# Weight conversion of a three-stage layer pair: whole tiles, sums on VectorE, and a held second layer

## The chip, the cores and the metric

The kernel runs on one core of one Trainium2 chip. The metric is the device time of one execution in microseconds (us). Before the change it is 1002.57 us, the median of 3 runs (1000.18 to 1002.59).

## The reference, cut to what matters

A linear attention gives x of 2304 tokens by 512, and two gated layers follow it. All data is float32.

```python
q_s = softmax(q, over d);  k_s = softmax(k, over s)      # 4 batches, 8 heads, 576 tokens, d = 64
x = (q_s @ (k_s^T @ v)) -> [2304, 512]
g = x @ w_gate; x = (g * sigmoid(g) * (x @ w_val)) @ w_out       # layer 0: 512 -> 1536 -> 512
x = ((x @ w_a) * (x @ w_b)) @ w_out2                             # layer 1: 512 -> 1536 -> 512
```

## The kernel before, in words

**Numbers as pairs.** TensorE multiplies operands of a shortened float format (fp32r). So every float32 operand is split into a high part (the rounded value, written by a cast on ScalarE) and a low part (the rest, a subtraction on VectorE or GpSimd), and every product takes three matmuls. x becomes `xhl`, the gated product becomes `h`, the weights become `w`.

**Where the weights come from.** Each weight matrix lies in HBM as 64-bit words, of which the kernel reads both 32-bit halves as integers. A part of the weights goes through a conversion of eight instructions (lines 367 to 388): on ScalarE `Abs` of the high words into `a` (L367, which VectorE may do instead, L369) and a scaling of the low words in place (L371); on VectorE a clamp (L373), a shift and mask (L376) and a merge with the sign (L379); then an exact integer sum of `a` and the low words (L384, on GpSimd, or on VectorE); then the cast to the high part of `w` on ScalarE (L302) and the subtraction to the low part of `w` (L296). The raw words are called `wr`.

**Tiles.** The 1536 hidden columns are 12 tiles of 128. Tile f of a layer holds 128 columns of both first matrices and 128 rows of the third: 1536 converted columns per partition. It is converted in two halves of 768 columns (tile 0 of layer 0 in three thirds of 512). Raw words of a half lie in one of the buffers `wr0`, `wr1` and, for most of layer 0, `xraw`; those of tiles 1 to 4 of layer 0 lie whole in tile buffers that are still free, so that they are loaded early. `a` has three buffers `a0`, `a1`, `a2` of one half each. A converted tile of layer 1 goes where the same tile of layer 0 was.

**Blocks.** The tokens are five blocks: four of 512 and a last one, block 4, of 256 (the rest rows of all four batches). Layer 0 runs blocks 0, 1, 2, 4, 3, layer 1 runs 0 to 4. In a block, each tile f gives two products `u` (24 matmuls, L743; L728 for the very first tile), and then, one tile later, `acc` takes the third product (12 matmuls, L770 or L773). Between them ScalarE makes `s` from the first product (L754), VectorE multiplies (L757), ScalarE casts to `h` (L302) and VectorE subtracts for its low part (L296). The two `u` products use two PSUM buffers; one is free again when `s` has read it, the other when the low part of `h` has been written. Block 0 of layer 0 is the one in which tiles are converted while they are used, and in which the attention of batch 1 also runs (four groups; `tm`, `kx`, `kr`, `kb`, `ut`, `kv`, `qt`, `ql`, `xt`, `xl` are its steps).

**Order.** All instructions are handed to a planner (class `Plan`), each with an engine, a cost, buffers that it reads and writes, and perhaps a due time or a second engine (`other`). The planner works due times back from the end (`prepare`, L95), then fills each engine in turn with what is ready and most urgent (`order`, L115). What it gives is a fixed queue for each engine, and every engine works its queue strictly in order. A step with a second engine goes there if the planner expects it to finish sooner (L140). The planner lets only one of VectorE and GpSimd work at a time for steps marked `port` (L136). Loads are issued by SyncE (SP) and are chained in the order in which they are written (`load`, L311). The conversion of layer 1 is written at L849, ahead of layer 1's first block, and the planner may start its loads and its steps up to the sum whenever buffers are free.

## Time and profile before

| | before |
|---|---|
| median of 3 runs | 1002.57 us |
| the profiled execution | 1002.42 us, of which 1000.5 us is the span |
| TensorE busy | 961.3 us (96%), mean granted clock 0.99 |
| VectorE, ScalarE, GpSimd busy | 402.0, 409.2, 172.2 us |
| sums on GpSimd (L384) | 48 of 49 |

The span runs from the first to the last instruction. "Busy" counts what an engine spends in an instruction, also while the instruction itself is held up. An entry in square brackets in a timeline is the idle time of the engine ahead of the instruction, with what ended it. Blocks of layer 0 begin at about 33 us (block 0), 172 us (block 1), 396 us (block 4) and 451 us (block 3).

### The profile page before, as it was taken

To read this page: it belongs to the slowest core of one execution; us is meant where nothing else is said; L and a number is where in the kernel's file an instruction comes from. 1 tells how busy PE (TensorE), PEld (TensorE's weight loads), DVE (VectorE), ACT (ScalarE), POOL (GpSimd) and SP (SyncE) were. 2 spreads that over 40 slices of the span, in tenths; PEclk is the share of its full clock that TensorE was granted. 3 is DMA by queue.
4 is the path that set the end of the run, shared out by engine and by line. 5 is a ranking of instruction groups with operands and counts; after the bars stand their busy time and mean duration, and the time that the engine had idled before them with its cause. 6 is when DMAs were issued, how large, how long until landed. Compare 5 with 4: busy or idle time off the path is not lost.

```text
span 1000.5 us, 12235 instructions
## 1 busy us (share of the span) xinstructions
PE 961.3 (96%) x4616; PEld 796.3 (80%) x4616; DVE 402.0 (40%) x693; ACT 409.2 (41%) x796; POOL 172.2 (17%) x193
## 2 busy tenths in 40 slices
PE   5699899999999999999999999999999999999997
PEld 4477677888888888898888888888888888888897
DVE  7988885332333233324566761211122112211211
ACT  5898986554454544223445441211121112111211
POOL 5655442100000001100444440000000000000000
PEclk9989899999999999999999999999999999999999
DMA  9825533211121114402334630010010001000100
GB/s 274 283 72 152 171 120 116 77 48 48 37 96 48 48 48 133 143 1 65 125 127 129 209 95 1 24 61 1 1 48 38 1 0 51 13 1 1 43 1 22
DMA packets 77138, 74.19 MB, mean 74 GB/s; under 512 B 29976, under 2 KB 64280, under 8 KB 76184
## 3 DMA queue, kind: packets, MB, share of 16 engines
q1 hardware_dynamic: 71416, 69.36, 22.4%
q10 hardware_dynamic: 5664, 4.07, 1.3%
q8 instruction: 36, 0.59, 0.3%
q14 instruction: 22, 0.18, 0.1%
HBM read 60.29 MB, written 13.11 MB: 73 GB/s over the span
## 4 chain that ended last, share of the span: by engine, by line
PE 83%; DMA 4%; ACT 4%; SPq 3%; DVE 2%; POOL 2%; issue 1%; POOLq 0%; DVEq 0%; ACTq 0%
PE u L743 53%; PE acc L773 15%; PE acc L770 12%; POOL a L384 2%; DMA ut<-in_k_dram 1%; DMA wr<-in_moe_w_gate_dram 1%; DMA wr<-in_moe_w_out_dram 1%; SPq L345 1%; PE kv L616 1%; PE xt L677 1%; DVE a L379 1%; SPq L504 1%; ACT L754 1%; ACT L601 1%; ACT a L367 0%
## 5 line engine op out<-in xcount | busy, mean ns | idle before, releaser
L743 PE MATMUL u<-xhl,w 128*128 128x512 f32 (+1 forms) x2856 | 624.4, 373 | 11.2 <-DVE w L296 7.2
L743 PEld LDWEIGHTS u<-xhl,w 128*128 128x128 f32 x2856 | 498.8, 189 | 109.4 <-DVE w L296 9.8
L757 DVE TENSOR_TENSOR u<-s,u 128x512 f32<-128x512 f32 (+1 forms) x120 | 77.1, 642 | 411.1 <-PE u L743 383.6
L754 ACT ACTIVATE s<-u 128x512 f32<-128x512 f32 (+1 forms) x120 | 66.8, 557 | 274.6 <-PE u L743 274.2
L770 PE MATMUL acc<-h,w 128*128 128x512 f32 (+1 forms) x720 | 165.2, 376 | 1.1 <-ACT ob L786 0.8
L773 PE MATMUL acc<-w,h 128*128 128x512 f32 x648 | 157.4, 392 | 0.0
L770 PEld LDWEIGHTS acc<-h,w 128*128 128x128 f32 x720 | 123.9, 188 | 28.5 <-issue 1.9
L302 ACT CAST h<-u 128x512 fp32r<-128x512 f32 (+1 forms) x120 | 65.0, 542 | 190.2 <-DVE u L757 188.0
L773 PEld LDWEIGHTS acc<-w,h 128*128 128x128 f32 x648 | 120.9, 188 | 25.6
L384 POOL TENSOR_TENSOR a<-a,wr 128x768 uint32<-128x768 uint32 (+1 forms) x48 | 95.2, 1984 | 177.5 <-DVE a L379 162.2
L296 DVE TENSOR_TENSOR h<-u,h 128x512 fp32r<-128x512 f32 (+1 forms) x120 | 76.3, 636 | 55.7 <-ACT h L302 55.5
L296 POOL TENSOR_TENSOR xhl<-xraw,xhl 128x512 fp32r<-128x512 f32 (+1 forms) x6 | 7.2, 1196 | 354.0 <-ACT xhl L302 239.9
L379 DVE SCALAR_TENSOR_TENSOR a<-wr,a 128x768 uint32<-128x768 uint32 (+1 forms) x49 | 52.0, 1062 | 0.5
L754 ACT ACT_TABLE_LOAD x26 | 33.4, 1283 | 29.2 <-PE u L743 29.0
L371 ACT ACTIVATE wr<-wr 128x768 uint32<-128x768 uint32 (+1 forms) x49 | 43.9, 897 | 3.0 <-DMA wr<-in_moe_w_out_dram 3.0
L302 ACT CAST w<-a 128x768 fp32r<-128x768 f32 (+1 forms) x49 | 39.9, 816 | 10.1 <-POOL a L384 6.2
L367 ACT ACTIVATE a<-wr 128x768 f32<-128x768 f32 (+1 forms) x38 | 33.7, 893 | 19.0 <-DMA wr<-in_moe_w_out_dram 15.2
L296 DVE TENSOR_TENSOR w<-a,w 128x768 fp32r<-128x768 f32 (+1 forms) x37 | 39.1, 1061 | 5.6 <-ACT w L302 4.0
L373 DVE TENSOR_SCALAR a<-a 128x768 f32<-128x768 f32 (+1 forms) x49 | 31.2, 639 | 20.7 <-ACT a L367 20.5
L376 DVE TENSOR_SCALAR a<-a 128x768 uint32<-128x768 uint32 (+1 forms) x49 | 30.3, 623 | 0.8
L296 POOL TENSOR_TENSOR w<-a,w 128x768 fp32r<-128x768 f32 (+1 forms) x12 | 22.5, 1875 | 17.4 <-ACT w L302 17.4
L601 ACT ACTIVATE ua<-uq,st 128x64 f32<-128x64 f32 (+1 forms) x72 | 24.6, 344 | 0.1
(107 smaller groups left out, 451.7 us busy)
## 6 DMA issues: line engine op xcount, KB each, us to landing
wr<-in_moe_w_out_dram SPq DMA_DIRECT2D x46, 256.0 KB, 4.4
xraw<-x SPq DMA_DIRECT2D x7, 1024.0 KB
wr<-in_moe_w_a_dram SPq DMA_DIRECT2D x24, 256.0 KB, 2.9
wr<-in_moe_w_b_dram SPq DMA_DIRECT2D x24, 256.0 KB, 3.0
wr<-in_moe_w_gate_dram SPq DMA_DIRECT2D x22, 256.0 KB, 5.8
wr<-in_moe_w_val_dram SPq DMA_DIRECT2D x22, 256.0 KB, 4.6
x<-ob SPq DMA_DIRECT2D x16, 256.0 KB, 2.1
out_dram<-ob SPq DMA_DIRECT2D x16, 256.0 KB, 3.4
```

The source lines that it names most:

```text
L296: engine.tensor_tensor(out=out(), in0=x(), in1=y(), op=op)
L302: add("scalar", act_us(n), lambda: nc.scalar.copy(out=hi(), in_=src()), [src_key], [hi_key])
L367: add("scalar", act_us(e) + 0.08, lambda: nc.scalar.activation(out=a().bitcast(F32), in_=high().bitcast(F32), func=AF.Abs), parts, [a], ot ...
L371: add("scalar", act_us(e) + 0.08, lambda: nc.scalar.activation(out=low(), in_=low(), func=AF.Copy, scale=2.0 ** -29), parts, [(raw, (h, "l ...
L379: add("vector", dve_us(e), lambda: nc.vector.scalar_tensor_tensor(out=a(), in0=high(), scalar=0xC0000000, in1=a(), op0=ALU.bitwise_and, op ...
L384: engine.tensor_tensor(out=a(), in0=a(), in1=low(), op=ALU.add)
L601: add("scalar", act_us(width) + 0.1, lambda: nc.scalar.activation(out=out(), in_=qraw()[:, at:at + width], func=AF.Exp, bias=st()[:, 0, x: ...
L743: nc.tensor.matmul(ps()[:, 0:n], lhsT=wv[:, c, :], rhs=x()[:, xs, c, 0:n], start=(a == 0 and c == 0), stop=(a == 2 and c == KD - 1))
L754: add("scalar", act_us(n), lambda: nc.scalar.activation(out=s()[:, 0:n], in_=ga()[:, 0:n], func=AF.Silu if l == 0 else AF.Copy), [ga], [s] ...
L757: add("vector", dve_us(n), lambda: nc.vector.tensor_tensor(out=gb()[:, 0:n], in0=s()[:, 0:n], in1=gb()[:, 0:n], op=ALU.mult), [s, gb], [gb])
L770: nc.tensor.matmul(ps()[:, 0:n], lhsT=w()[:, 4 + ws, o * P:(o + 1) * P], rhs=h()[:, hs, 0:n], start=begin, stop=end)
L773: nc.tensor.matmul(ps(), lhsT=h()[:, hs, o * P:(o + 1) * P], rhs=w()[:, 4 + ws, :], start=begin, stop=end)
```

## The change

A tile of layer 0 with number 1 to 4 is now converted whole: clamp, shift, merge, sum, cast and subtraction are one instruction each over 1536 columns, and so are `Abs` and the scaling. Such a tile's `a` has 1536 columns and lies in `a0` or in `xraw`; the third `a` buffer is gone, so that halves have `a0` and `a1`. The integer sum has VectorE as its first engine and GpSimd as its second. The first load of layer 1 gets an order (`hold`) behind the first product of block 3 of layer 0, which does not count for due times; as all loads are chained, all of layer 1's loads lie behind it.

```diff
     def add(self, engine, cost, fn, reads=(), writes=(), due=None, after=(), table=None, nbytes=0, other=None,
-            port=None):
+            port=None, hold=()):
...
-        deps, order, allocs = set(), set(after), []
+        deps, order, allocs = set(), set(after) | set(hold), []
...
             for s in self.succ[n]:
+                if n in ops[s]["hold"]:
+                    continue
...
     def load(fn, nbytes, writes, issue=0.475):
-        n = dma(fn, nbytes, [], writes, after=last_load, issue=issue)
+        n = dma(fn, nbytes, [], writes, after=last_load, issue=issue, hold=tuple(not_before))
         last_load[:] = [n]
+        not_before.clear()
...
-    WR, AT = ("wr0", "wr1"), ("a0", "a1", "a2")
-    RAW = WR + ("xraw",)
+    WR, AT = ("wr0", "wr1"), ("a0", "a1")
+    WHOLE = ("a0", "xraw")
...
-    def convert(l, f, c, ms, c0, c1, spare, raw=None):
+    def convert(l, f, runs, raw=None):
...
+        w, u32 = w_t[l, f], Buf(sp, [P, sum(len(run[2]) for run in runs), len(runs[0][1]), WH], U32,
+                              WHOLE if len(runs) > 1 else AT, f"a{l}_{f}_{runs[0][0]}")
...
-        add("vector", dve_us(e, 2), lambda: nc.vector.tensor_scalar(
+        add("vector", dve_us(size, 2), lambda: nc.vector.tensor_scalar(
             out=a().bitcast(F32), in0=a().bitcast(F32), scalar1=TOP, scalar2=LEAST,
-            op0=ALU.min, op1=ALU.max), [a], [a], port=True)
+            op0=ALU.min, op1=ALU.max), every, every, port=True)
...
-        add("gpsimd", pool_us(e), lambda: whole(nc.gpsimd), [a, (raw, (h, "low"))], [a],
-            other=("vector", dve_us(e), lambda: whole(nc.vector), True))
+            add("vector", dve_us(e), lambda total=total: total(nc.vector), [*A1, (r, (cs[0], "low"))], A1,
+                other=("gpsimd", pool_us(e), lambda total=total: total(nc.gpsimd), True), port=True)
...
     def convert_tile(l, f):
-        spare, raw = l == 0 and f < NF - 2, None
+        runs, raw = [(h, [0, 1, 2], [h]) for h in range(2)], None
         if l == 0 and f <= AHEAD:
-            raw = Buf(wp, [P, 2, 3, WC // 2, 2], U32, f"w{f + NF - KD - AHEAD - 1}", f"wr{l}_{f}")
-        for h in range(2):
-            list(convert(l, f, h, [0, 1, 2], h * WC // 2, (h + 1) * WC // 2, spare, raw))
+            raw = Buf(wp, [P, 2, 3, WH, 2], U32, f"w{f + NF - KD - AHEAD - 1}", f"wr{l}_{f}")
+            list(convert(l, f, runs, raw))
+        else:
+            for run in runs:
+                list(convert(l, f, [run]))
...
         if (l, i) == (1, 0):
+            not_before.extend(begun)
             for f in range(NF):
                 convert_tile(1, f)
...
             ga, gb = ups(l, i, f, x)
+            if (l, i, f) == (0, B - 1, 0):
+                begun = main["last"]
```

The queue of VectorE after the cast of tile 1, before the change. Names are those of the code, with a number of the build behind them; `a_2_0` and `a_2_1` are the halves of tile 2, `wr_2` its raw words, and `tm` and `h_0_0` are what TensorE waits for there.

```order
L757 TENSOR_TENSOR u_0_0_1_412<-s_0_0_457,u_0_0_1_412 128x512
L575 TENSOR_REDUCE st_493<-ut_410 128x8
L373 TENSOR_SCALAR a_2_1_485<-a_2_1_485 128x768
L376 TENSOR_SCALAR a_2_0_465<-a_2_0_465 128x768
L376 TENSOR_SCALAR a_2_1_485<-a_2_1_485 128x768
L379 SCALAR_TENSOR_TENSOR a_2_0_465<-wr_2_255,a_2_0_465 128x768
L379 SCALAR_TENSOR_TENSOR a_2_1_485<-wr_2_255,a_2_1_485 128x768
L296 TENSOR_TENSOR tm_525<-ut_410 128x2x2x64
L296 TENSOR_TENSOR h_0_0_511<-u_0_0_1_412,h_0_0_511 128x512
```

The same place of VectorE's queue after the change, as far as the second step of `ut`; lines are those of the new file, and an `ISA` row is the integer sum (it counts 16-bit halves, so 128x3072 is 1536 columns).

```order
L779 TENSOR_TENSOR u_0_0_1_409<-s_0_0_453,u_0_0_1_409 128x512
L298 TENSOR_TENSOR tm_471<-ut_400 128x2x2x64
L382 TENSOR_SCALAR a_3_0_478<-wr_3_316 128x1536
L387 TENSOR_SCALAR a_2_0_467<-a_2_0_467 128x1536
L298 TENSOR_TENSOR h_0_0_489<-u_0_0_1_409,h_0_0_489 128x512
L578 TENSOR_REDUCE kr_502<-kx_492 128x1
L597 TENSOR_REDUCE st_511<-ut_400 128x8
L390 TENSOR_SCALAR a_2_0_467<-a_2_0_467 128x1536
L600 TENSOR_REDUCE st_511<-ut_400 128x1
L396 SCALAR_TENSOR_TENSOR a_2_0_467<-wr_2_255,a_2_0_467 128x1536
L298 TENSOR_TENSOR ut_400<-ut_400,kb_540 128x2x4x64
L401 ISA a_2_0_467<-wr_2_255,a_2_0_467 128x3072
```

`tm` now stands directly behind the first product's multiplication and `h_0_0` behind two wide steps, and tile 2's sum is in this queue and not in GpSimd's.

The queue of ScalarE where layer 0 passes from block 2 to block 4, before (`s_4_1` and `h_4_1` belong to tile 1 of block 4, `ob_2_2` is a copy of block 2's result, and `a_1_0`, `wr_1_1` are halves of layer 1's tile 1).

```order
L302 CAST h_4_0_3331<-u_4_0_1_3294 128x256
L754 ACTIVATE s_4_1_3334<-u_4_1_0_3313 128x256
L302 CAST h_4_1_3363<-u_4_1_1_3338 128x256
L786 COPY ob_2_2_3368<-acc_2_2_2517 128x512
L367 ACTIVATE a_1_0_3390<-wr_1_0_3323 128x768
L371 ACTIVATE wr_1_0_3323<-wr_1_0_3323 128x768
L754 ACTIVATE s_4_2_3404<-u_4_2_0_3381 128x256
L371 ACTIVATE wr_1_1_3366<-wr_1_1_3366 128x768
```

The same place after the change.

```order
L776 ACTIVATE s_4_0_3246<-u_4_0_0_3224 128x256
L808 COPY ob_2_2_3257<-acc_2_2_2481 128x512
L304 CAST h_4_0_3270<-u_4_0_1_3241 128x256
L776 ACTIVATE s_4_1_3277<-u_4_1_0_3259 128x256
L304 CAST h_4_1_3305<-u_4_1_1_3279 128x256
L776 ACTIVATE s_4_2_3333<-u_4_2_0_3315 128x256
L304 CAST h_4_2_3353<-u_4_2_1_3328 128x256
L776 ACTIVATE s_4_3_3377<-u_4_3_0_3359 128x256
```

Layer 1's steps have left this place; on SP the loads of layer 1 now stand behind the four stores of block 4's result (`x_4`), and on GpSimd 36 of 48 integer sums are gone.

## Rows read from the trace of the kernel before

**Rows 1.** Busy time by stage; columns: length, engines busy (instructions), clock, DMA, GB/s
```profile
36.00:97.00 61.00, 53.08 (x234) 41.17 (x233) 53.29 (x82) 53.33 (x101) 36.77 (x36) 0.94 0.44 130
97.00:165.00 68.00, 60.48 (x263) 47.00 (x262) 51.09 (x79) 53.28 (x100) 28.52 (x29) 0.95 0.49 154
...
390.00:420.00 30.00, 27.51 (x200) 25.41 (x199) 13.84 (x26) 13.57 (x26) 6.35 (x4) 1.00 0.64 212
...
460.00:600.00 140.00, 140.00 (x614) 114.75 (x613) 91.86 (x125) 68.72 (x97) 55.20 (x28) 1.00 0.39 123
```

**Rows 2.** Waits of TensorE, 36 to 165 us: total, times, longest
```profile
PE u L743 <- DVE w L296: 7.2, 5, 2.8
PE kx L553 <- DVE tm L296: 4.9, 1, 4.9
...
PE ql L667 <- ACT ut L671: 1.2, 1, 1.2
```

**Rows 3.** Timeline of TensorE in block 0: start, duration, line, count, [idle before]
```profile
43.76 2.56 PE L743 MATMUL u<-xhl,w 128*128 128x512 f32 x10 [0.88 <-DVE w L296]
51.20 0.69 PE L553 MATMUL kx<-ident,tm 128*128 128x128 f32 x2 [4.88 <-DVE tm L296]
...
59.33 2.01 PE L743 MATMUL u<-xhl,w 128*128 128x512 f32 x8
...
102.34 5.42 PE L743 MATMUL u<-xhl,w 128*128 128x512 f32 x22 [0.89 <-DVE w L296]
...
114.28 7.44 PE L743 MATMUL u<-xhl,w 128*128 128x512 f32 x18 [2.81 <-DVE w L296]
...
161.17 4.16 PE L743 MATMUL u<-xhl,w 128*128 128x512 f32 x17 [1.42 <-DVE w L296]
```

**Rows 4.** Busy time in two microseconds behind the longest idle time of tile 7
```profile
116.00:118.00 2.00, 2.00 (x6) 1.52 (x6) 2.00 (x4) 2.00 (x6) 1.84 (x1) 0.50 0.00 0
```

**Rows 5.** Timeline of VectorE in block 0
```profile
49.10 2.04 DVE L296 TENSOR_TENSOR tm<-ut 128x256 f32<-128x256 f32 x1
...
70.59 0.55 DVE L373 TENSOR_SCALAR a<-a 128x768 f32<-128x768 f32 x1
71.06 0.95 DVE L379 SCALAR_TENSOR_TENSOR a<-wr,a 128x768 uint32<-128x768 uint32 x1
71.93 0.55 DVE L376 TENSOR_SCALAR a<-a 128x768 uint32<-128x768 uint32 x1
72.40 0.68 DVE L296 TENSOR_TENSOR h<-u,h 128x512 fp32r<-128x512 f32 x1
73.00 2.04 DVE L379 SCALAR_TENSOR_TENSOR a<-wr,a 128x768 uint32<-128x768 uint32 x1
...
101.33 0.96 DVE L296 TENSOR_TENSOR w<-a,w 128x768 fp32r<-128x768 f32 x1 [0.37 <-ACT w L302]
...
146.30 0.96 DVE L384 CUSTOM_DVE_ANT_0 a<-wr,a 128x1536 uint16<-128x1536 uint16 x1
```

**Rows 6.** Timeline of GpSimd in block 0
```profile
48.45 4.40 POOL L384 TENSOR_TENSOR a<-a,wr 128x768 uint32<-128x768 uint32 x2 [0.73 <-DVE a L379]
...
72.14 2.08 POOL L384 TENSOR_TENSOR a<-a,wr 128x768 uint32<-128x768 uint32 x1 [5.37 <-DVE a L379]
```

**Rows 7.** Timeline of ScalarE, tile 6 of block 0 and block 4
```profile
90.03 0.93 ACT L367 ACTIVATE a<-wr 128x768 f32<-128x768 f32 x1 [2.03 <-DMA wr<-in_moe_w_out_dram]
...
410.50 0.88 ACT L371 ACTIVATE wr<-wr 128x768 uint32<-128x768 uint32 x1 [2.99 <-DMA wr<-in_moe_w_out_dram]
411.29 0.36 ACT L302 CAST h<-u 128x256 fp32r<-128x256 f32 x1
```

**Rows 8.** Timeline of TensorE in block 4 of layer 0
```profile
401.19 1.70 PE L743 MATMUL u<-xhl,w 128*128 128x256 f32 x12 [0.53 <-ACT s L754]
...
412.16 1.70 PE L743 MATMUL u<-xhl,w 128*128 128x256 f32 x12 [1.17 <-DVE h L296]
```

**Rows 9.** The integer sum's line: count, shortest/median/longest ns, first and last start
```profile
L384 POOL TENSOR_TENSOR a<-a,wr x48: 1297/1886/2571, 23.4 to 599.5; 128x768 uint32<-128x768 uint32 x45, 128x512 uint32<-128x512 uint32 x3
```

More of the change, by code (lines that the diff above doesn't have):

```diff
@@ L337, in convert @@
             w_parts[l, f] = {m: [] for m in range(3)}
-        w = w_t[l, f]
-        parts = [(raw, (h, x)) for x in range(n)]
-        for x, m in enumerate(ms):
-            w_parts[l, f][m].append(c)
-            def get(x=x, m=m):
-                if m < 2:
-                    nc.sync.dma_start(
-                        out=rows()[:, x].rearrange("p (c n) t -> p c (n t)", n=P),
-                        in_=mats[l][m][:, f * 2 * P:(f + 1) * 2 * P].rearrange(
-                            "(c p) n -> p c n", p=P)[:, c0 // P:c1 // P, :])
-                else:
-                    nc.sync.dma_start(
-                        out=rows()[:, x].rearrange("p n t -> p (n t)"),
-                        in_=mats[l][m][f * P:(f + 1) * P, 2 * c0:2 * c1])
-            load(get, P * width * 8, [(raw, (h, x))])
@@ L371, in convert, with a @@
-        add("scalar", act_us(e) + 0.08, lambda: nc.scalar.activation(
-            out=low(), in_=low(), func=AF.Copy, scale=2.0 ** -29), parts, [(raw, (h, "low"))])
-        add("vector", dve_us(e, 2), lambda: nc.vector.tensor_scalar(
+        keys = [c for c, *_ in runs]
+        if raw is not None:
+            bits = [(raw, lambda: raw(), keys, runs[0][1], [0, 1])]
+        size = (h1 - h0) * (m1 - m0) * WH
+        every = [(u32, c) for c in keys]
+        def a(halves=None):
+            return u32() if halves is None or len(runs) == 1 else u32()[:, halves[0]:halves[-1] + 1]
@@ new lines, in convert @@
+        for r, rows, cs, ms, halves in bits:
+            e, A1 = len(ms) * len(halves) * WH, [(u32, c) for c in cs]
+            R1 = [(r, (c, x)) for c in cs for x in range(len(ms))]
+            add("scalar", act_us(e) + 0.08, lambda rows=rows, halves=halves: nc.scalar.activation(
+                out=a(halves).bitcast(F32), in_=rows()[..., 1].bitcast(F32), func=AF.Abs), R1, A1,
+                other=("vector", dve_us(e, 2), lambda rows=rows, halves=halves: nc.vector.tensor_scalar(
+                    out=a(halves), in0=rows()[..., 1], scalar1=0x7FFFFFFF, scalar2=None,
+                    op0=ALU.bitwise_and), True))
+            add("scalar", act_us(e) + 0.08, lambda rows=rows: nc.scalar.activation(
+                out=rows()[..., 0], in_=rows()[..., 0], func=AF.Copy, scale=2.0 ** -29), R1, [(r, (cs[0], "low"))])
@@ L379, in convert @@
-        add("vector", dve_us(e), lambda: nc.vector.scalar_tensor_tensor(
-            out=a(), in0=high(), scalar=0xC0000000, in1=a(),
-            op0=ALU.bitwise_and, op1=ALU.bitwise_or), [a, *parts], [a], port=True)
-        def whole(engine):
-            engine.tensor_tensor(out=a(), in0=a(), in1=low(), op=ALU.add)
-        add("gpsimd", pool_us(e), lambda: whole(nc.gpsimd), [a, (raw, (h, "low"))], [a],
-            other=("vector", dve_us(e), lambda: whole(nc.vector), True))
-        split(lambda: part(0), lambda: part(1), lambda: a().bitcast(F32), e, (w, (c, 0)), (w, (c, 1)), a)
+            op0=ALU.logical_shift_left, op1=ALU.bitwise_and), every, every, port=True)
@@ new lines, in convert, with total @@
+        for r, rows, cs, ms, halves in bits:
+            e, A1 = len(ms) * len(halves) * WH, [(u32, c) for c in cs]
+            R1 = [(r, (c, x)) for c in cs for x in range(len(ms))]
+            add("vector", dve_us(e), lambda rows=rows, halves=halves: nc.vector.scalar_tensor_tensor(
+                out=a(halves), in0=rows()[..., 1], scalar=0xC0000000, in1=a(halves),
+                op0=ALU.bitwise_and, op1=ALU.bitwise_or), [*A1, *R1], A1, port=True)
+            def total(engine, rows=rows, halves=halves):
+                engine.tensor_tensor(out=a(halves), in0=a(halves), in1=rows()[..., 0], op=ALU.add)
+            add("vector", dve_us(e), lambda total=total: total(nc.vector), [*A1, (r, (cs[0], "low"))], A1,
+                other=("gpsimd", pool_us(e), lambda total=total: total(nc.gpsimd), True), port=True)
@@ L390, in convert_tile @@
+        his, los = [[(w, (c, t)) for c in keys] for t in range(2)]
+        add("scalar", act_us(size), lambda: nc.scalar.copy(out=part(0), in_=a().bitcast(F32)), every, his)
+        pair(size, lambda: part(1), lambda: a().bitcast(F32), lambda: part(0).bitcast(F32), ALU.subtract,
+             [*every, *his], los)
     def convert_tile(l, f):
-        spare, raw = l == 0 and f < NF - 2, None
+        runs, raw = [(h, [0, 1, 2], [h]) for h in range(2)], None
         if l == 0 and f <= AHEAD:
-            raw = Buf(wp, [P, 2, 3, WC // 2, 2], U32, f"w{f + NF - KD - AHEAD - 1}", f"wr{l}_{f}")
@@ L823 @@
     units = [attend(0, g, xhl, None) for g in range(KD)]
-    tile0 = [convert(0, 0, m, [m], 0, WC, True) for m in range(3)]
+    tile0 = [convert(0, 0, [(m, [m], [0, 1])]) for m in range(3)]
     for u in units:
```

55 lines of the change are left out of this document (31 added, 24 removed).

## The prediction, as it was put on record before the changed kernel ran

> **What bounds the kernel now.** I read the stages first. Between 460 and 600 us TensorE is busy for the whole 140 us while layer 1 is converted beside it [rows 1]. So nothing can be won there; it can only be lost. TensorE falls short in two places. In block 0 of layer 0, from 36 to 165 us, it is busy 53.1 of 61 and 60.5 of 68 us: 15.4 us idle. In the 30 us around block 4 it is idle for 2.5 us [rows 1].
>
> Next I read what ended these waits. In block 0, 7.2 us are waits for the low part of a weight tile, and 4.9 us is one wait for `tm` [rows 2]. They lie at 43.8, 51.2, 102.3, 114.3 and 161.2 us, and more between [rows 3]. The long ones cost twice: behind the wait that ends at 114.28 the clock is granted at 0.50, 1.2 instead of 2.4 GHz [rows 4]. The mean clock of 0.94 over 61 us and 0.95 over 68 us [rows 1] stands for some 7 us at half rate in each stretch; in part of that TensorE idled anyway, so I put the loss at 2 and 3 us. So 20 us is all that block 0 can give back.
>
> Last I read the engines that are waited for. VectorE and ScalarE are each busy 53 of 61 us, then 51 and 53 of 68 [rows 1], so this block is bound by the conversion. Part of VectorE's time is no work: the merge of 768 columns takes 0.95 us at 71.06, but 2.04 us at 73.00, when a GpSimd sum runs from 72.14 to 74.22 [rows 5, 6]. The subtraction for `h` at 72.40, which has one operand in PSUM, took its 0.68 us in the middle of that sum. `tm`, a step of 256 columns, takes 2.04 us at 49.10, beside two GpSimd sums that together take 4.40 us [rows 5, 6].
>
> **Durations.** From start to start, a merge of 768 columns takes 0.87 us and a clamp or shift 0.47; a step of 512 takes 0.60 [rows 5]. That is 1.05 ns a column and 0.06 us fixed. I take 0.87 us for a clamp or shift of 1536 columns and 1.67 for a merge, sum or subtraction. One sum was done on VectorE: 0.96 us [rows 5], against 1.89 on GpSimd in the median [rows 9]. That single row carries all sums that move. Their price can hardly be under the 0.81 us that 768 columns take at 1.05 ns, nor over the 1.89 of GpSimd.
>
> The sum reads every second 32-bit word, as the merge does, which took 0.95 us [rows 5]. By the Trainium skill, "Vector Engine (DVE) Microarchitecture Reference", section "Measured stream behaviour on trn2", that should be slow: an SBUF port runs at full rate only on runs of two or more adjacent words, and one source that hops at every element gives 1.73 ns a column. By that a sum of 768 columns would take an estimated 1.4 us, the 17 that move to VectorE in block 0 would cost it 8 us more, and of the 9 us that I forecast below 1 would be left. Both rows contradict it, and the measurement decides.
>
> **What moves in block 0.** Fewer instructions alone are worth little: a whole tile saves six of VectorE's starts at 0.06 us, 1.4 us over four tiles. The engine of the sum is worth more. By the queues, GpSimd does 24 sums and 6 weight subtractions in layer 0 before and 7 and 4 after. So 17 sums and 2 subtractions leave, about 36 us of the resource that both engines block, and VectorE takes on about 17 us of work (17 x 0.9 and 2 x 0.87): the shared time falls by 19 us. VectorE itself gets no emptier, since its 17 us of new work replaces about as much time stuck behind GpSimd. What shortens is the chain of one half: two queue changes fewer, and 0.9 instead of 2 us.
>
> Against that stand two costs. A whole tile cannot begin before both halves have come, and its wide steps hold up the short ones behind them by up to 1.67 us. And `a` has two buffers for halves and not three.
>
> I walked the four queues by hand from 30 us, with those durations. `w_1` is ready at about 42.7 instead of 43.76 [rows 3]. `tm` stands behind one short step and no longer behind two merges and two sums, so `kx` follows at about 45.5 instead of 51.20 [rows 3]. The second product of tile 1 needs the PSUM buffer that `h_0_0` frees; that comes at about 48.2 behind a clamp of 1536 columns. By here 4 us are won, and the halved clock at 51 us perhaps avoided. Then they are spent. Tile 2 has VectorE full with its shift, merge, sum and `ut`, and TensorE reaches the first product of tile 2 at about 58.1, against 59.33 [rows 3], with `kv` already done (1.2 us). The planner gives both products of tile 2 the same PSUM buffer, so that the second waits for `s` on ScalarE, 2 us. At tile 5 I am 1.4 us ahead, at tile 6, whose raw words need a buffer that an earlier sum frees, 2.9 us: 99.4 against 102.34 [rows 3]. First term: 2.9 us. Its bounds are 7 us gained (all that the wait for `tm` and its clock cost) and 2 us lost (the steps behind the wide ones).
>
> From tile 6 to tile 11 TensorE now needs (161.17 - 102.34) / 5 = 11.8 us a tile [rows 3], of which 8.2 us are its own 36 matmuls (140 us / 614 each [rows 1]); some of the rest are the attention's products. The waits in there are those for `w` but the first two, 7.2 - 0.9 - 0.9 = 5.4 us, and 1.2 us for `ql` [rows 2, 3]; with 3 us of clock that is 9.6. Here the halves are as narrow as before; what changes is the sum's engine. VectorE's work per tile then comes to 2 x (0.47 + 0.47 + 0.87 + 0.96 + 0.87) = 7.3 us for the halves, 1.2 for `u` and `h` and about one for the attention. That is 9.5 us, about TensorE's own pace, so I expect to get half of the 9.6 back and not all. Second term: 4.8 us. Its bounds are 9.6 gained and, if the two buffers decide, a loss (the third rival).
>
> **The hold.** In block 4 a conversion of layer 1 stands in the way three times. The clearest: the scaling at 410.50 waits 2.99 us for its load, `h` stands behind it at 411.29, and TensorE waits until 412.16 [rows 7, 8]. The waits at 401 and 412 are 0.53 and 1.17 us [rows 8]; with a third, for a copy of block 2's result, they make the 2.5 us of that stretch [rows 1]. After the change none of these steps is left in that queue. What is late next: the copies of block 2's result, two of which wait for a store to free their buffer; one of them has moved behind `h_4_1` on VectorE. I leave 0.3 us for it. Third term: 2.2 us, between 0 and 2.5.
>
> What the hold costs is hidden. The loads of layer 1 start behind the stores of block 4 on SP, so after 451 us. Nothing of layer 1 can be written to its tile before block 3 has used that tile, so only the steps up to the sum, of three to four halves, come later. With 8.2 us a tile, layer 1 starts at about 550 us and comes to its tile 11 at 640. The last sum started at 599.5 [rows 9]. The 140 us from 460 on hold some 21 halves, 6.7 us each, so four more make it 626 at that pace, with 14 us to spare. VectorE has 92 of 140 us in that stretch [rows 1], and GpSimd's part falls. So I put it at 0. If that cover went, each wait would cost TensorE its length: 0 to 3 us.
>
> **Sum.** 2.9 + 4.8 + 2.2 = 9.9 us. I take 0.9 off for the second term, whose half is a choice. 1002.4 of the profiled execution (1000.5 of span) minus 9.0 is 993.4; the median of the runs shown is 0.15 above that execution, so 993.5.
>
> **Rivals.** First, VectorE becomes the bound of block 0. For it: 17 us of work move to an engine that is busy in 53 of 61 us [rows 1]. Against it: much of that time is waiting for GpSimd [rows 5, 6]. Then the first two terms are 0 and only block 4 is left: 1002.4 - 2.2 = 1000.2, no change that can be told.
>
> Second, all comes free: the wait for `tm` goes with its clock, and tiles 6 to 11 run at TensorE's pace. That is 7 + 9.6 or somewhat less, say 15, plus 2.2: 985.
>
> Third, slower: two buffers for `a` pace the tiles. A half of tile f+1 can begin only when the same half of tile f has been subtracted, so a tile takes as long as one half's chain. That chain took from 90.03 [rows 7] to 102.29 [rows 5], 12.3 us, for tile 6 before, with three buffers to spread it. If VectorE's longer queue makes it 14 us, tile 11 starts at 99.4 + 5 x 14 = 169.4, 8.2 us late, and with block 4 the time is 1008.4. It decides from (161.17 + 2.2 - 99.4) / 5 = 12.8 us on. Against it: the chain loses a GpSimd sum of 2 us and stalls of 1 us, which leaves 9 to 11 us.
>
> That the change does not do what it says is small: 12 sums stay on GpSimd, but the queues show the rest moved.
>
> **Chances.** Forecast (988 to 998) 0.52, only block 4 0.19, all free 0.17, slower 0.12. A measurement of this kernel can tell 0.3%, 3.0 us, from no change. Faster by more: 0.52 + 0.17 + 0.04 of the first rival = 0.73; within it 0.15; slower 0.12. The range 986 to 1001.5 leaves the slower case and part of the free one out; the forecast's own is 988 to 998.
>
> **What would show it.** The wait for `tm` near 51 us gone and a new one before tile 2's products, for `kv` or `w_2`; sums on VectorE at 0.96 and about 1.7 us, merges no longer at 2 us; TensorE's idle time between 36 and 165 us down from 15.4 to about 9; the first product of tile 11 about 7 us earlier; no idle time in block 4 beyond 0.5 us; none between 460 and 600. I am wrong if sums take 1.4 us or more, if tiles 6 to 11 keep 11.8 us a tile, or if TensorE waits for tiles of layer 1.

## The result: 9.8 us less, and the profile after

The changed kernel takes 991.67 us (median of four runs, 991.02 to 992.62) where the kernel before takes 1001.49 (four runs, 1000.18 to 1002.59). The ratio is 0.9903 with a 95% interval of 0.9885 to 0.9921. 993.5 had been forecast, between 986 and 1001.5. The two profiled executions lie 11.4 us apart (1002.42 and 991.02, spans of 1000.5 and 989.2); 1.6 of that comes from which executions were profiled: one 0.9 above its median, the other 0.65 below. What is read from this one pair of profiles carries that difference.

The same four stages, in columns as in [rows 1], of the changed kernel:

```profile
36.00:97.00 61.00, 56.42 (x254) 44.72 (x253) 56.83 (x80) 52.35 (x94) 18.82 (x26) 0.97 0.49 147
97.00:165.00 68.00, 62.48 (x288) 50.05 (x287) 55.64 (x95) 55.08 (x117) 14.75 (x18) 1.00 0.48 150
390.00:420.00 30.00, 29.00 (x244) 28.60 (x242) 6.72 (x16) 5.29 (x14) 0.00 (x0) 1.00 0.09 37
460.00:600.00 140.00, 140.00 (x614) 114.86 (x613) 105.60 (x143) 75.42 (x105) 24.12 (x13) 1.00 0.42 134
```

TensorE's idle time in block 0 fell from 15.4 to 10.1 us [rows 1], its clock rose from 0.94 and 0.95 to 0.97 and 1.00, and GpSimd's work halved. VectorE is busy for 8 us more. Layer 1 still does not hold TensorE up. Before 36 us, a stretch that the stages of the prediction leave out, TensorE is now idle for 1.84 us more; first before, then after:

```profile
0.00:36.00 36.00, 21.03 (x101) 16.21 (x102) 26.89 (x62) 22.30 (x43) 22.09 (x35) 0.95 1.02 301
```
```profile
0.00:36.00 36.00, 19.19 (x96) 14.70 (x96) 26.75 (x60) 21.08 (x39) 22.69 (x39) 0.95 1.01 297
```

Where the 11.3 us of the spans came from is read off the same products in both timelines of TensorE: the first of tile 6 and of tile 11 in block 0, the first of block 4 of layer 0, one of the last of that block, the last of all. Before:

```profile
100.73 0.72 PE L743 MATMUL u<-xhl,w 128*128 128x512 f32 x2
...
159.11 0.63 PE L743 MATMUL u<-xhl,w 128*128 128x512 f32 x2
...
396.19 4.47 PE L743 MATMUL u<-xhl,w 128*128 128x256 f32 x36
...
447.62 1.77 PE L770 MATMUL acc<-h,w 128*128 128x256 f32 x14
...
992.07 2.92 PE L773 MATMUL acc<-w,h 128*128 128x512 f32 x12
```

After, with the second product of tile 1 and the wait ahead of tile 2 in front, and block 4's one wait:

```profile
46.36 0.38 PE L575 MATMUL kx<-ident,tm 128*128 128x128 f32 x2
...
47.24 2.99 PE L765 MATMUL u<-xhl,w 128*128 128x512 f32 x12 [0.39 <-DVE h L298]
...
55.63 2.10 PE L638 MATMUL kv<-ut 128*128 128x130 f32 x8 [2.49 <-ACT ut L616]
...
57.81 3.45 PE L765 MATMUL u<-xhl,w 128*128 128x512 f32 x12
...
97.48 3.00 PE L765 MATMUL u<-xhl,w 128*128 128x512 f32 x12
...
151.92 5.62 PE L765 MATMUL u<-xhl,w 128*128 128x512 f32 x24
...
386.69 6.17 PE L765 MATMUL u<-xhl,w 128*128 128x256 f32 x48
...
394.89 0.62 PE L792 MATMUL acc<-h,w 128*128 128x256 f32 x3 [1.00 <-DVE ob L808]
...
436.37 1.77 PE L792 MATMUL acc<-h,w 128*128 128x256 f32 x14
...
980.75 2.92 PE L795 MATMUL acc<-w,h 128*128 128x512 f32 x12
```

At tile 6 the changed kernel is 3.25 us ahead (100.73 - 97.48), at the start of block 4 9.50, near its end 11.25, and at the last product 11.32. So 3.25 us were won by the first product of tile 6, 6.25 from there to block 4, 1.75 in block 4, and layer 1 gives or costs nothing. (The forecast set its mark at tile 6 a little later, which is taken up below.)

The waits in block 0 (total, times, longest), against [rows 2]:

```profile
PE kv L638 <- ACT ut L616: 4.2, 2, 2.5
PE u L765 <- DVE h L298: 1.6, 2, 1.2
PE ql L689 <- DVE ut L650: 1.5, 1, 1.5
PE xt L699 <- ACT ut L693: 1.1, 1, 1.1
PE u L765 <- DVE w L298: 1.1, 1, 1.1
...
PE u L750 <- DVE w L298: 0.3, 1, 0.3
```

The waits for the low part of `w` are down from 7.2 us to 1.4 and the one of 4.9 for `tm` is gone. In their place TensorE waits for the attention's steps on ScalarE and VectorE, such as `ut` for `kv`.

How long VectorE was held up can be added up from the traces: for each of its steps that starts between 36 and 165 us, the time above the median of the same operation and shape in all runs, where it is over 0.1 us. That is 15.5 us before the change and 2.7 us after it.

### The profile page after: what moved, and what is told of

Its sections match the earlier page's. It is cut to its first block, busy times and chain, and to the rows that moved or that the text cites. A ratio compares the mean times of both kernels' runs of the same rounds, so it can differ in the third digit from the quotient of the medians.

```text
span 989.2 us, 12151 instructions
## 1 busy us (share of the span) xinstructions
PE 955.1 (97%) x4616; PEld 794.2 (80%) x4616; DVE 417.3 (42%) x708; ACT 402.8 (41%) x780; POOL 104.5 (11%) x158
## 4 chain that ended last, share of the span: by engine, by line
PE 91%; DMA 3%; DVE 2%; ACT 1%; SPq 1%; issue 1%; POOL 0%; DVEq 0%; ACTq 0%; POOLq 0%
PE u L765 58%; PE acc L795 15%; PE acc L792 14%; PE xt L699 1%; PE kv L638 1%; DMA ut<-in_q_dram 1%; DMA wr<-in_moe_w_out_dram 1%; DMA wr<-in_moe_w_gate_dram 1%; DMA wr<-in_moe_w_val_dram 0%; DMA x<-xq 0%; SPq L526 0%; PE qt L686 0%; ACT wr L385 0%; SPq L351 0%; DMA ut<-in_k_dram 0%
## 5 line engine op out<-in xcount | busy, mean ns | idle before, releaser
L396 DVE SCALAR_TENSOR_TENSOR a<-wr,a 128x768 uint32<-128x768 uint32 (+2 forms) x45 | 51.2, 1137 | 0.8
L406 ACT CAST w<-a 128x768 fp32r<-128x768 f32 (+2 forms) x45 | 39.3, 874 | 17.5 <-DVE a L401 13.1
L385 ACT ACTIVATE wr<-wr 128x768 uint32<-128x768 uint32 (+2 forms) x45 | 43.0, 957 | 1.4 <-DMA wr<-in_moe_w_out_dram 1.4
L380 ACT ACTIVATE a<-wr 128x768 f32<-128x768 f32 (+2 forms) x35 | 33.4, 954 | 14.5 <-DMA wr<-in_moe_w_out_dram 8.1
L401 POOL TENSOR_TENSOR a<-a,wr 128x768 uint32<-128x768 uint32 (+1 forms) x12 | 23.0, 1916 | 148.7 <-DVE a L396 106.6
L401 DVE CUSTOM_DVE_ANT_0 a<-wr,a 128x1536 uint16<-128x1536 uint16 (+1 forms) x33 | 34.7, 1052 | 1.7
L298 DVE TENSOR_TENSOR w<-a,w 128x768 fp32r<-128x768 f32 (+2 forms) x32 | 33.1, 1044 | 2.8 <-ACT w L406 2.7
L387 DVE TENSOR_SCALAR a<-a 128x768 f32<-128x768 f32 (+2 forms) x45 | 28.5, 634 | 6.0 <-ACT a L380 5.6
L390 DVE TENSOR_SCALAR a<-a 128x768 uint32<-128x768 uint32 (+2 forms) x45 | 26.7, 594 | 0.8
```

The costliest lines, as they stand in the source:

```text
L298: engine.tensor_tensor(out=out(), in0=x(), in1=y(), op=op)
L380: add("scalar", act_us(e) + 0.08, lambda rows=rows, halves=halves: nc.scalar.activation(out=a(halves).bitcast(F32), in_=rows()[..., 1].bit ...
L385: add("scalar", act_us(e) + 0.08, lambda rows=rows: nc.scalar.activation(out=rows()[..., 0], in_=rows()[..., 0], func=AF.Copy, scale=2.0 * ...
L396: add("vector", dve_us(e), lambda rows=rows, halves=halves: nc.vector.scalar_tensor_tensor(out=a(halves), in0=rows()[..., 1], scalar=0xC00 ...
L401: engine.tensor_tensor(out=a(halves), in0=a(halves), in1=rows()[..., 0], op=ALU.add)
L406: add("scalar", act_us(size), lambda: nc.scalar.copy(out=part(0), in_=a().bitcast(F32)), every, his)
```

## The experiments

Theory A, that of the prediction: the sum's engine makes the gain of block 0, since a sum on VectorE shortens a half's chain and stops stalling VectorE's other steps; the hold makes that of block 4. Theory B: the whole tiles make the gain of block 0. Theory C: any edit gives the planner another order, and the gain is such an order. Each of the twelve was timed five or more times beside the kernel before on the same chip; e1 to e4, e5 to e8, e9 to e11 and e12 ran on four different chips, so that between these groups the ratios compare better than the medians.

| kernel | sums first on | tiles 1-4 | `a` buffers | hold | median us | ratio to before, 95% interval | block 4 begins at | idle 36-165 |
|---|---|---|---|---|---|---|---|---|
| before | GpSimd | halves | 3 | no | 1001.49 | 1 | 396.2 | 15.4 |
| changed | VectorE | whole | 2 | yes | 991.67 | 0.9903 (0.9885-0.9921) | 386.7 | 10.1 |
| e4 | VectorE | halves | 3 | no | 994.15 | 0.9930 (0.9917-0.9942) | 388.9 | 10.0 |
| e5 | GpSimd | whole | 2 | no | 1007.34 | 1.0056 (1.0037-1.0075) | 401.6 | 18.6 |
| e6 | GpSimd | halves | 3 | yes | 1000.25 | 0.9986 (0.9974-0.9998) | 394.9 | 13.6 |
| e2 | GpSimd | whole | 2 | yes | 1006.42 | 1.0054 (1.0041-1.0067) | 403.5 | 18.1 |
| e1 | VectorE | halves | 3 | yes | 995.26 | 0.9938 (0.9926-0.9950) | 388.0 | 9.4 |
| e3 | VectorE | whole | 2 | no | 993.03 | 0.9912 (0.9898-0.9926) | 387.8 | 9.2 |
| e7 | VectorE only | whole | 2 | yes | 994.15 | 0.9926 (0.9908-0.9944) | 389.2 | 11.3 |
| e8 | VectorE | halves | 2 | no | 997.90 | 0.9965 (0.9952-0.9978) | 392.4 | 15.1 |
| e9 | VectorE | whole, in raw buffers | 3 | yes | 1003.05 | 1.0017 (1.0008-1.0026) | 396.3 | 15.9 |
| e10 | as before, `SLACK` 0.8 | | | | 1007.39 | 1.0059 (1.0046-1.0072) | 397.6 | 14.5 |
| e11 | as changed, `SLACK` 0.8 | | | | 994.48 | 0.9926 (0.9912-0.9940) | 390.4 | 11.2 |
| e12 | as e9, `xraw` kept free | | | | 1001.06 | 0.9998 (0.9985-1.0010) | 398.3 | 16.3 |

The last two columns are of the one profiled execution. Idle time alone does not order the kernels: e1, e3 and e4 idle no longer than the changed kernel, but in each of them the granted clock from 97 to 165 us is 0.97, where the changed kernel's is 1.00.

The hold does not touch block 0. Up to the end of that block VectorE, ScalarE and GpSimd work through the same steps in the same order in before and e6, in e4 and e1, in e5 and e2, and in the changed kernel and e3. So these pairs show how far two executions of one order lie apart there (0.9 to 1.9 us at the start of block 4), and the table has fewer orders of block 0 than rows.

**e4, the sums alone.** The kernel before with the two engines of the sum exchanged. It is written as the changed kernel with halves and three buffers (as in e1 below) and without the line `not_before.extend(begun)`, so that this part of the change is what is left:

```diff
-            add("gpsimd", pool_us(e), lambda total=total: total(nc.gpsimd), [*A1, (r, (cs[0], "low"))], A1,
-                other=("vector", dve_us(e), lambda total=total: total(nc.vector), True))
+            add("vector", dve_us(e), lambda total=total: total(nc.vector), [*A1, (r, (cs[0], "low"))], A1,
+                other=("gpsimd", pool_us(e), lambda total=total: total(nc.gpsimd), True), port=True)
```

> The kernel before with one edit: the integer sum on VectorE first (16 sums stay on GpSimd instead of 48); halves, three buffers for a, no hold. Theory A: 994, that is 7 to 8 us of the 9.8: all but block 4. Theory B: 998 to 1001. Rival (VectorE becomes the bound of block 0): 1001.5, no change.

994.15 us. Theory A's number came; by the ratios 7.0 of the 9.7 us, some seven tenths of the gain, come with this one edit. That VectorE would be the bound and nothing change, the first rival of the prediction, is out.

**e2 and e5, the sums back on GpSimd.** The reverse edit in the changed kernel; e5 also drops the line `not_before.extend(begun)`, so that the whole tiles stand alone.

> The changed kernel with the integer sum on GpSimd first again (45 of the sums there instead of 12); whole tiles and the hold stay. Theory A: 997 to 1000, since the first two terms are the sum's engine: the idle time of TensorE between 36 and 165 us is back at 13 us or more, with merges of VectorE of 2 us or more beside sums on GpSimd. Theory B: 993 to 995, idle time near 10 us. Theory C: no order in it.

> The kernel before with one edit: tiles 1 to 4 converted whole, with a0 and a1 for a; sums on GpSimd first (45 there), no hold. Theory A, after the run with GpSimd first: whole tiles pay only where VectorE does the sums, since a sum of 1536 columns on GpSimd lasts 3.5 to 3.9 us, stands in the chain of the whole tile and holds up VectorE's steps for as long; so 1005 to 1009, slower than before, with idle times for w of 2 to 3 us at tiles 2 and 5. Theory B (whole tiles pay by themselves, what the undoing of them cost): 997. Rival: the hold made the run with GpSimd first slow, and without it: 1001.

Both are slower than before. For e2 theory A had said 997 to 1000, and so A as first stated is wrong too: the sum's engine is not all. e5 is where A, by then corrected, had put it. B as it stands is out: whole tiles, which come with two `a` buffers here, cost 6 us where GpSimd sums (1007.34 against 1001.2 beside it, 1006.42 against 1000.25). The trace of e2 shows one way in which they do, on GpSimd, VectorE and TensorE in turn:

```profile
37.40 3.91 POOL L401 TENSOR_TENSOR a<-a,wr 128x1536 uint32<-128x1536 uint32 x1 [4.06 <-DMA wr<-in_moe_w_gate_dram]
```
```profile
39.10 2.58 DVE L387 TENSOR_SCALAR a<-a 128x512 f32<-128x512 f32 x1
41.71 0.43 DVE L390 TENSOR_SCALAR a<-a 128x512 uint32<-128x512 uint32 x1
```
```profile
60.88 1.95 PE L765 MATMUL u<-xhl,w 128*128 128x512 f32 x4 [2.74 <-DVE w L298]
```

A sum of a whole tile holds GpSimd for 3.91 us, until 41.31, and a clamp of 512 columns that starts beside it lasts 2.58 us, until 41.68; the shift right behind it, of the same size and past the sum, takes 0.43. So the clamp did its work when the sum had ended. The wide sum stands in the chain of the whole tile besides: TensorE waits for `w` of tile 2 before 60.88, where the changed kernel has no wait for `w`. In e5 the same wait is 5.14 us. How much of the 6 us is the wide sums, and how much the third buffer that is missing or the other order, no run tells: halves with two buffers and the sums on GpSimd were not run.

**e1, halves again.** The changed kernel with `convert_tile` calling `convert` once for each half and `AT` with three buffers.

```diff
-    WR, AT = ("wr0", "wr1"), ("a0", "a1")
+    WR, AT = ("wr0", "wr1"), ("a0", "a1", "a2")
...
-        if raw is not None:
+        if raw is not None and len(runs) > 1:
...
-            list(convert(l, f, runs, raw))
-        else:
-            for run in runs:
-                list(convert(l, f, [run]))
+        for run in runs:
+            list(convert(l, f, [run], raw))
```

> The changed kernel with tiles 1 to 4 converted in halves again (and three buffers for a again): the sums on VectorE first and the hold stay. Theory A (the sum's engine makes the gain of block 0: 17 sums leave GpSimd, the chain of a half loses two queue changes, VectorE's merges no longer stall): 992, between 991 and 994, because whole tiles save only six starts of an instruction each. Theory B (the whole tiles make it: six short steps fewer are in the way of the attention's steps, and the wait for tm at 51 us goes by that): 995 to 998, with an idle time of 3 to 5 us before kx near 50 us. Theory C (every edit only gives the planner another order, and the parts do not add up): anything from 990 to 1000.

995.26 us: theory A's 992 was wrong, the time is B's, but without B's wait for `kx`. Of the 3.3 us between the two spans (992.5 and 989.2) 1.3 lie ahead of block 4; idle time does not make them (9.4 us against 10.1 between 36 and 165 us), the lower clock does (0.97 against 1.00 from 97 us on). Of the other 2.0, 1.5 us is one wait in layer 1, for an `h` that stands behind a clamp of layer 1's conversion (1.68 us, beside a GpSimd subtraction): the hold's cover is gone there. The row is of TensorE in e1:

```profile
549.84 3.02 PE L763 MATMUL u<-xhl,w 128*128 128x512 f32 x12 [1.52 <-DVE h L298]
```

**e3 and e6, the hold.** The hold taken from the changed kernel (the line `not_before.extend(begun)` left out), and put alone into the kernel before.

> The changed kernel without the hold: the loads of layer 1 may be issued before block 3 of layer 0. Theory A: 993.5, 1.8 us more than the changed kernel, with idle times for h or s behind conversion steps of layer 1 in block 4 again, and block 0 as in the changed kernel to within 0.5 us. Rival: the sum's engine alone takes the conversion of layer 1 out of the way in block 4, and the hold is worth nothing: 991.7. Theory C: another order also in block 0, anything.

> The kernel before with one edit: the hold. Theory A: block 0 as before, 1.8 us less in block 4, no or up to 2 us of new waits in layer 1 near 550 to 600 us, because 36 sums and more of layer 1 still go to GpSimd: 999 to 1001. Rival, by the run with halves, in which TensorE waited 1.5 us in layer 1: the hold costs more than it gives where a tile comes in halves: 1001 to 1004.

e6: from the start of block 4 (394.88) to its last large group of products it now takes 1.7 us less, as in theory A, and TensorE waits for nothing between 460 and 600 us; the median moves by 1.0, with an interval that just leaves out zero. In e3 the wait for `h` of 1.17 us at 412.16 [rows 8] is gone without the hold; the waits left in block 4 are those for `s` and a copy, 1.32 us together. By the ratios the hold gives 1.4 us (before to e6), 0.2 (e5 to e2) and 0.9 (e3 to the changed kernel), and costs 0.8 from e4 to e1; each of these is less than another order can move (below).

Its own stretch shows it better. From the start of its first matmul of `u` to that of its last of `acc`, block 4 takes 52.4 to 52.8 us in all eight kernels with the hold and 53.2 to 57.5 in the six without it. But what it is worth there depends on the sums: 1.75 us from before to e6, 1.0 from e3 to the changed kernel and 0.4 from e4 to e1. As the wait for `h` goes with the sums alone, only about 1.0 of the 1.75 us that the change won in block 4 is the hold's. And it has a price in layer 1: waits of 1.5 us at its start in e1, e9 and e12 and 0.2 in e7, but none in the changed kernel, e2, e6 and e11.

**e8, two buffers.** e4 with `AT = ("a0", "a1")`.

> The kernel with the sums on VectorE first alone (994.2 us), with two buffers for a instead of three. Theory A (the chain of one half lasts 9 to 11 us and two buffers do not pace TensorE at 11 us a tile): 993 to 995.5. Rival (the third rival of the prediction, two buffers pace the tiles): 998 to 1004, with tiles 6 to 11 at 12 us and more.

The rival was nearly right in the price, 3.7 us more than with three buffers and 0.1 under its range, and wrong in the place. TensorE in e8:

```profile
55.02 0.41 PE L573 MATMUL kx<-ident,tm 128*128 128x128 f32 x2 [2.31 <-DVE tm L298]
...
62.22 2.93 PE L763 MATMUL u<-xhl,w 128*128 128x512 f32 x6 [4.89 <-DVE w L298]
```

The loss lies at tiles 1 and 2, not at tiles 6 to 11, where e8 is not idle for more than 1.3 us at a time and goes at 10.8 us a tile. So the change gave its third buffer up for the whole tiles, and from e8 to e3 those returned 4.9 us, about as much as another order alone can move.

**e7, no sum on GpSimd.** The changed kernel with `other=` left out of the sum.

> The changed kernel with every integer sum on VectorE (none of the last 12 on GpSimd). Theory A (what GpSimd's sums block is worth more than VectorE's time): the same or a little better, 989 to 992. Rival (VectorE is the bound of block 0 by now, busy in 56.8 of 61 us): 994 to 997, with more idle time between 36 and 165 us, and waits in layer 1.

994.15 us, 2.5 more than the changed kernel. That is at the edge of the rival's range and, by the next pair, no more than another order moves by itself. Whether VectorE's time or the order did it stays open; more sums off GpSimd brought nothing.

**e10 and e11, another order alone.** One number of the planner, in both kernels:

```diff
-    SLACK = 0.7
+    SLACK = 0.8
```

> The kernel before with one number of the planner changed, its allowance for a change of queue in the due times 0.8 us instead of 0.7: no work is changed, moved to another engine on purpose or given another buffer, only the order of the queues differs. It tells how much of a difference any new order makes. Theory A (the gain comes from the sums): 999 to 1003. Theory C (any new order moves the time by several us, and the change's gain is such an order): as likely under 998 or over 1005 as between.

> The changed kernel with the same number of the planner changed, 0.8 instead of 0.7 us. Theory A: 990 to 995, the gain over the kernel before with that number staying 7 to 12 us. Theory C: the gain falls under 5 us or rises over 14.

The kernel before loses 5.6 us by its chance order and the changed one 2.8. For the first that is as theory C said, and it sets the measure: 5.6 us between two orders is no evidence for a cause by itself. With 0.8 the gain of the whole change is 12.9, between the 7 to 12 of theory A and the over 14 of theory C.

The trace says where e10's loss lies. Block 4 begins only 1.4 us later than before; inside it TensorE waits once, 3.73 us, for a copy that stands on ScalarE behind a step of layer 1 and then waits for a store, and the clock behind it is 0.50:

```profile
408.68 1.34 PE L770 MATMUL acc<-h,w 128*128 128x256 f32 x6 [3.73 <-ACT ob L786]
```

That block takes 57.54 us in e10 and 54.55 before. So 3 of the 4.6 us between the two spans belong to the stretch in which the hold acts, and ahead of block 4 another order moved the kernels by 1.4 us (e10) and 3.7 (e11).

For A speaks that the exchange of engines won in all four pairs that differ by it alone: 7 us (before and e4), 5 (e6 and e1), 14 (e5 and e3), 15 (e2 and the changed kernel). In block 0 these are two comparisons, halves and whole tiles, each measured twice; there the exchange brings the start of block 4 forward by 7.3 and 6.9 us with halves and by 13.8 and 16.8 with whole tiles, more than another order moved it. VectorE's time above the median, added up as for the result, agrees: 14.5 to 16.6 us in e2, e5, e6 and e10, which sum on GpSimd, and 2.7 to 11.3 in the others. A short stall is not enough, though: e9 has 6.5 us and is no faster than before.

**e9 and e12, a version to beat both.** Whole tiles held in raw buffers, three buffers for the halves; in e12 `xraw` is also kept from the raw words of tiles 5 and 6.

```diff
-    WR, AT = ("wr0", "wr1"), ("a0", "a1")
-    WHOLE = ("a0", "xraw")
+    WR, AT = ("wr0", "wr1"), ("a0", "a1", "a2")
+    WHOLE = ("wr0", "wr1", "xraw")
```

In e12 alone, the buffers that the raw words of a half may take (only this part of the line is shown):

```diff
-WR + ("xraw",) if l == 0 and f < NF - 2 else WR
+WR + ("xraw",) if l == 0 and f < NF - 2 and f not in (5, 6) else WR
```

> The changed kernel with the third buffer for a back: whole tiles are held in wr0, wr1 or xraw, which tiles 1 to 4 don't need for their raw words, and a0, a1 and a2 are left to the halves. Theory A (the change paid some 3.7 us for its whole tiles with the third buffer, as the run with two buffers for halves showed): 988 to 991, better than the changed kernel's 991.7. Rival 1 (the third buffer decides only where tiles 1 to 4 come in halves too; the whole ones have their own place already): 991 to 993. Rival 2 (raw words of tile 5 and 6 then wait for these buffers): 993 to 997.

> The kernel with the third buffer and whole tiles in raw buffers (1003.1 us), with xraw kept from the raw words of tiles 5 and 6. In that kernel the first step of tile 4 started at 77.24 us, behind both halves of tile 5, which held xraw, and TensorE waited 6.40 us for its w before 90.61. Theory A (a buffer taken out of turn made tile 4 late): that wait goes, or falls under 2 us, and with its two windows at half clock the time comes to 993 to 997. Rival 1 (the early tiles lose as much: TensorE's waits of 3.21 and 2.13 us at 47 and 58 us stay, and with them the time): 998 to 1001. Rival 2 (the wait only moves to tiles 5 and 6, which get their raw words later): 1001 to 1005.

Neither beat the changed kernel. In e9 VectorE starts tile 4 late and subtracts it behind tile 5 (widths 768 are tile 5's halves, 1536 is tile 4), and TensorE waits:

```profile
77.24 1.89 DVE L382 TENSOR_SCALAR a<-wr 128x1536 uint32<-128x1536 uint32 x1 [1.79 <-POOL a L401]
79.05 0.94 DVE L298 TENSOR_TENSOR w<-a,w 128x768 fp32r<-128x768 f32 x1
...
87.37 0.95 DVE L298 TENSOR_TENSOR w<-a,w 128x768 fp32r<-128x768 f32 x1
...
88.79 1.76 DVE L298 TENSOR_TENSOR w<-a,w 128x1536 fp32r<-128x1536 f32 x1
```
```profile
90.61 8.20 PE L765 MATMUL u<-xhl,w 128*128 128x512 f32 x24 [6.40 <-DVE w L298]
```

In the changed kernel the same subtraction starts at 72.76. e12 gave tile 4 a place, and that wait fell to 3.34 us, not under 2; waits of 3.20 at 47.00 and others early in the block stayed, as rival 1 had it, and the time fell by 2.0 us only, to 1001.06, at the upper edge of that rival. (The profile of e12 is of its slowest execution, 1004.51.) With its buffers given out in another way the planner began tile 5 ahead of tile 4 in e9, and the tile due next was late.

## Why the prediction was right, step by step

The number came, and the path of the first term was the one walked; its size was less well met, and part of the second term was luck.

**First term, 2.9 us forecast, 4.3 measured at its own mark.** `kx` came at 46.36 (45.5 forecast), the second product of tile 1 at 47.24 (48.2), then the new wait before tile 2's products, and tile 2's first product at 57.81 (58.1). The forecast's mark was the group of tile 6 that begins at 102.34, behind the wait for `w` [rows 3]; the same matmuls begin at 98.03 in the changed kernel, inside the group at 97.48. So the term measures 4.3 us (the 3.25 above are read at the tile's first product, ahead of that wait) and was forecast 1.4 us too small. This is the mis-sized term. Nearly all of the 1.4 is there already at tile 5, where the walk had 1.4 us won and 2.7 were (90.25 before, 87.51 after). Two more parts were off. The walk began at 30 us and missed a loss of 1.8 us before 36. VectorE and TensorE there, in the changed kernel:

```profile
32.00 1.49 DVE L387 TENSOR_SCALAR a<-a 128x1536 f32<-128x1536 f32 x1
33.41 0.15 DVE L645 RECIPROCAL ks<-ks 128x2 f32<-128x2 f32 x1
33.52 0.96 DVE L390 TENSOR_SCALAR a<-a 128x1536 uint32<-128x1536 uint32 x1
34.52 0.29 DVE L650 TENSOR_SCALAR ut<-kv,ks 64x64 f32<-64x64 f32 x1
```
```profile
34.95 1.10 PE L699 MATMUL xt<-ut 128*128 128x512 f32 x2 [1.43 <-DVE ut L650]
```

The clamp and shift of whole tile 1 stand ahead of a step of 0.15 and one of 0.29 us, and TensorE waits 1.43 us for the latter's `ut`: the cost that the prediction gave wide steps, in a place it had not looked at. On the other side, the second half of tile 2 waited 0.34 us for `s` and not 2.

**Second term, 4.8 us forecast, 5.2 measured from the same mark** (6.25 from the tile's first product). I had let half of the 9.6 come back, idle time and clock alike. Of idle time less came, 2.0 of 7.5 us between 97 and 165 us; the clock came back whole, 0.95 to 1.00 over 68 us, which is at most 3.4 us. The long wait for `w` that ended at 114.28 [rows 3], with the half clock behind it [rows 4], is gone, and none of the waits left in that stretch (1.72 us at most) is followed by a lower clock in the profiled execution. That is in part luck. e3 works through the same steps in the same order, with the same waits of 1.46 and 1.14 us at 140.64 and 142.19 (140.86 and 142.40 in the changed kernel), and there the clock is 0.50 from 142 to 144 us. The stretch in e3:

```profile
97.00:165.00 68.00, 63.32 (x285) 50.32 (x284) 55.92 (x95) 55.76 (x118) 14.07 (x17) 0.97 0.49 150
```

Over the whole span, by the first line of each profile, before and after:

```profile
PE 961.3 (96%) x4616; PEld 796.3 (80%) x4616; DVE 402.0 (40%) x693; ACT 409.2 (41%) x796; POOL 172.2 (17%) x193
```
```profile
PE 955.1 (97%) x4616; PEld 794.2 (80%) x4616; DVE 417.3 (42%) x708; ACT 402.8 (41%) x780; POOL 104.5 (11%) x158
```

The same 4616 matmuls took 6.2 us less, so only 5.1 of the 11.3 us are idle time. The clock in the two stretches of block 0 makes at most 1.8 (0.03 of 61 us) and 3.4 us of the 6.2. TensorE was idle in part of the time at half clock, before 51.20 and before 114.28 above all; counted over its busy time there, the clock makes 0.7 and 3.1 us. The last 2 us or so I did not trace. Other executions differ less: the mean granted clock is 0.992 to 0.996 in the four of the changed kernel, of which the profiled one is the highest, and 0.987 to 0.993 in those of the kernel before that were timed beside the experiments.

Tiles 6 to 11 go at (151.92 - 97.48) / 5 = 10.9 us, against (159.11 - 100.73) / 5 = 11.7.

**The durations.** The sum's line in the changed kernel, with shortest, median and longest ns:

```profile
L401 DVE CUSTOM_DVE_ANT_0 a<-wr,a x33: 937/958/1753, 37.1 to 593.7; 128x1536 uint16<-128x1536 uint16 x29, 128x3072 uint16<-128x3072 uint16 x4
L401 POOL TENSOR_TENSOR a<-a,wr x12: 1291/1874/2712, 23.8 to 574.3; 128x768 uint32<-128x768 uint32 x9, 128x512 uint32<-128x512 uint32 x3
```

0.96 and 1.75 us a sum were forecast as 0.96 and 1.67, from one row. The stalls did not go wholly, since some sums and subtractions stayed on GpSimd: three merges of 768 columns in block 0 still last 1.23 to 1.86 us and two of layer 1's conversion last 2.5, against the forecast's "merges no longer at 2 us". VectorE's new work was to replace about as much time stuck; 12.8 us of that time went, and VectorE is busy for 8 us more. A merge of 768 columns on VectorE in the changed kernel, and the sum on GpSimd beside it:

```profile
114.64 1.86 DVE L396 SCALAR_TENSOR_TENSOR a<-wr,a 128x768 uint32<-128x768 uint32 x1
```
```profile
113.81 1.87 POOL L401 TENSOR_TENSOR a<-a,wr 128x768 uint32<-128x768 uint32 x1
```

The sum ends at 115.68 and the merge 0.82 us later, about the time it takes alone, as the one of 73.00 ended 0.82 us behind its sum before [rows 5, 6]. By the Trainium skill, "Vector Engine (DVE) Microarchitecture Reference", section "Measured stream behaviour on trn2", one source that hops 4 KiB at every element costs 1.73 ns a column, from which the prediction estimated 1.4 us a sum for words two apart. All 29 sums of 768 columns in the changed kernel contradict that estimate; the longest took 0.96 us.

**Third term, 2.2 us forecast, 1.75 measured.** The number came in part by another way than the hold: with the sums on VectorE the wait for `h` of 1.17 us goes without it (e3, e4). The copy of block 2's result behind `h_4_1` cost 1.00 us at 394.89, where 0.3 had been left for it; without the hold the same place has waits of 1.32 us (e3).

**Layer 1, 0 forecast, 0 measured**; e1, e9 and e12 show that the cover is thin, with 1.5 us lost in other orders.

**What the forecast had not seen.** It took the parts as terms that add. Alone they measure 7 us gained (sums), 6 lost (whole tiles) and 1 gained (hold), together 2; the change gained 9.8. The whole tiles, with the two buffers that go with them, change sign with the engine of the sum, though their 6 us are about what another order moved. Its second rival (15 us and more free) failed because the conversion leaves the attention's steps late: VectorE is busy for 93% of 36 to 97 us, and the `ut` of the longest wait left (2.49 us) stands on ScalarE behind the cast of whole tile 2, which had itself waited 0.98 us for VectorE's sum. Its third, two buffers that pace tiles 6 to 11, did not show: e8 lost 3.7 us, but at tiles 1 and 2.

The Trainium skill, "Perfetto Trace Analysis", section "Optimizing Scalar/DVE Operations", says two things that bear on this: larger operations pay where the engine is saturated, and, since GpSimd and VectorE share a read port, moving work from one to the other may not help. The runs fit both: with sums on VectorE first the larger operations won 1 to 4 us (e4 to e3, e1 to the changed kernel), which is within what another order moves, with sums on GpSimd first they cost 6, and the sums that had stood on GpSimd cost more there than on the busier VectorE.

## What to carry to other kernels

Before work is moved off a busy engine to a second one, look at whether the first one's rows get longer while the second works; here taking the work back won 5 to 15 us, though the busy engine was then busy for 8 us more. Make instructions wider only after that, since a wider one on the sharing engine stalls the other for longer (beside a sum of 3.91 us a clamp lasted 2.58). Where a planner sets the order, run it once with a neutral number changed: a gain smaller than what that moves (here 3 to 6 us) is no proof of a cause by its time alone. Then compare the stretch in which the edit acts; block 4 showed the hold where the whole times could not. A third buffer, with another place for the whole tiles, made this kernel 11 us slower.
